# Nine units instead of ten on the first half chunk, and weights split at column 1152

## The chip, the cores and the metric

The kernel runs on one core of one Trainium2 chip. The core has five engines that run their own instruction streams and meet at semaphores: PE (TensorE, matmuls and transposes into PSUM), ACT (ScalarE, activations and PSUM reads), DVE (VectorE, elementwise work and statistics), POOL (GpSimd) and SP (SyncE, which here only issues DMA). The metric is the device time of one execution in microseconds. Before the change it was 170.09 us, the median of 3 runs (169.66 to 171.05).

## The reference

With S = 2048 rows, D = 512 columns and an inner width of 1792, all in bf16:

```python
xn = (x - mean(x)) / sqrt(var(x) + 1e-5)            # over the 512 columns
A  = irfft2(rfft2(xn) * (w_r + 1j * w_i))           # over rows and columns
B  = (gelu(xn @ w_gate) * (xn @ w_up)) @ w_down     # 512 -> 1792 -> 512
out = x + A + B
```

A is a filter in the frequency domain, computed here by matmuls with cosine and sine tables and by elementwise folds. B is a gated feed-forward layer, and holds most of the matmuls.

## The kernel before, in words

**Tiling.** Row r of the kernel's text is a tile of 128 rows of x with all 512 columns; there are 16. Four of them are a chunk b (512 rows), so there are four chunks. A unit is one group of 128 of the 1792 inner columns, numbered fc = 0 to 13. For a unit and a chunk `gated` (L679 and on) computes the gate product g and the up product u, each as four matmuls over the 512 input columns (L688), then gelu of g on ACT (L693), a copy of u on ACT (L696), and their product hT on DVE (L699). `down` (L746) multiplies hT by w_down, 14 matmuls for each row of a chunk. For chunks 0 to 2 ACT and DVE add it into x (L754, L755); for the last chunk DVE adds it from PSUM (L757), and the result is stored.

**The first chunk.** It can't be computed whole at once, since its rows arrive one by one. Rows 0 and 1 are its first half, rows 2 and 3 its second. `by_rows` (L702 and on; matmuls L712, ACT L730 and L731, DVE L732) computes units for one row at a time, 128 columns per matmul, so that a row can begin before the next one is there. The first half is: units 0 to 2 row by row (rows 0 and 1), then units 3 to 9 with both rows at once (256 columns per matmul). The second half is units 0 and 1 row by row (rows 2 and 3), then units 2 to 9 with 256 columns. Units 10 to 13 follow with all four rows at once (512 columns). `NHALF` is the number of units that are done in halves, `NFIRST` (3) of them row by row at the start.

**PSUM.** The gu pool has three banks; a gated unit takes one for g and one for u. In `by_rows` a unit holds g and u in one bank, from gu or from the dn bank, which `down` uses later. The sp pool has two pairs of banks for transposes and spectral products, and for the last chunk's down products.

**Transposes.** The normalized row has to be transposed (xnT) to be a matmul operand. Rows 0 and 1 are transposed on PE (L542, L525). From row 2 on, `turn_dma` (L554) issues a transposing DMA on SP's queue once DVE has written the normalized row (L512). `mirror` (L569) transposes one more tile per chunk in the same way. `fold` builds the operands of the forward transform on DVE; PE transforms over columns at L596 with ACT evicting at L601, over tokens at L834 and L838, back at L915 and L916, and L975.

**The loads.** All on SP's queue in this order: rows 0 to 3, then w_gate and w_up by column ranges (384 to 768, 768 to 1024, 1024 to 1280; columns 0 to 384 come on ACT's queue), the transposes of rows 2 and 3, rows 4 to 7, the transpose of `mirror`, weights 1280 to 1792, rows 8 to 11, a table, rows 12 to 15, and later w_down and the rest. A packet is the run of one weight row, so 256 columns give 512 bytes, 384 give 768 and 512 give 1024.

**The planner.** The order of each engine's instructions is not written out by hand. `_Sched.run` simulates the kernel with fixed costs per operation when the program is built, and lists, for each engine, the operation that can start first, with keys and due times to break ties. DMAs share one pipe of 340 GB/s that starts at 3.3 us, with 0.4 us to land; some early landings are written in. Matmuls of the feed-forward part have keys in program order and fill PE wherever nothing else is ready. PE's spectral operations count as ready 1 us late (`MARGIN`). An `order` list forces one operation behind another on the same engine: ACT evicts the third by-rows unit (dn bank) behind the gelu of units 3 and 5. Nothing is reordered when the program runs.

Of the kernel before, what the change touches and what calls it, by code (L numbers as in the profile page):

```python
# [14 lines left out]
FF = 1792  # L15
P = 128
NFC = 14
NHALF = 10
NFIRST = 3
WARM = 10 * (512,) + (256,)  # L20
HKEY = 1.5
# [123 lines left out]
class _Sched:  # L145
# [11 lines left out]
    def op(self, eng, cost, fn, reads=(), writes=(), tiles=(), key=0.0, after=(), dma=0, lag=0.0, due=None, land=None):  # L157
        o = _Op()
        o.eng, o.fn, o.cost, o.key, o.dma, o.lag, o.due, o.land = eng, fn, cost, key, dma, lag, due, land
        o.reads, o.writes, o.tiles = reads, writes, [(t, False) for t in tiles]  # L160
        o.extra = [a for a in after if a is not None]
        o.order = []
        o.seq = len(self.ops)
        o.end = None
        o.pos = None
        self.ops.append(o)
        return o
# [165 lines left out]
def bass_parallel_sum__spectral_gfnet__glu_gated_geglu__prompt_kernel(  # L333
# [17 lines left out]
    wgv = B_w_gate.rearrange("(dc p) f -> p dc f", p=P)  # L351
    wuv = B_w_up.rearrange("(dc p) f -> p dc f", p=P)
# [5 lines left out]
    with ExitStack() as es:  # L358
        def sb(name, shape, dt=BF16, cell=0):
            n = int(np.prod(shape))  # L360
            t = es.enter_context(nc.sbuf_tensor(name, [P, n], dt))
            return view(t, name, 0, shape, cell)
# [15 lines left out]
        wg = sb("wg", [4, FF])  # L378
        wu = sb("wu", [4, FF])
# [39 lines left out]
        def gub(t, n=512):  # L419
            return ps_gu[:, t.slot * 512:t.slot * 512 + n]  # L420
# [8 lines left out]
        def mm(n):  # L429
            return max(0.0565, n * 0.000421)  # L430

        def c_tt(n):
            return 0.07 + n / 1920.0
# [4 lines left out]
        def c_act(n):  # L438
            return 0.05 + n * 0.00088
# [23 lines left out]
        def load(q, dst, src, nbytes, **kw):  # L463
            return dma(q, dst, lambda: src, nbytes, wr=(dst,), **kw)

        def wload(q, dst, src, lo, hi, **kw):
            return load(q, dst[:, :, lo:hi], src[:, :, lo:hi], (hi - lo) * 1024, **kw)

        k = iter(np.arange(0.0, 1.0, 0.001))
        def rows(lo, hi, land=None):  # L470
            return load("sp", x[:, lo:hi], xb[:, lo:hi, :], (hi - lo) * 131072, key=next(k), land=land)
# [6 lines left out]
        gate.append(warms[3])  # L478
        rows(2, 3, 6.9)
        rows(3, 4, 7.2)  # L480
        for lo, hi in ((384, 768), (768, 1024), (1024, 1280)):
            for w, v in ((wg, wgv), (wu, wuv)):
                wload("sp", w, v, lo, hi, key=next(k))
        op("pool", 0.1, lambda e: e.memset(eps.ap, LN_EPS), writes=(eps,), key=-2)
# [136 lines left out]
        gate.append(early)  # L621
        rows(4, 8)
        k = iter(np.arange(1.0, 2.0, 0.001))
        for w, v in ((wg, wgv), (wu, wuv)):
            wload("sp", w, v, 1280, FF, key=next(k))
        rows(8, 12)
        load("sp", small[:, 1:9].rs([8 * P]), c_small.ap()[:, P:], 262144, key=next(k))
        rows(12, 16)
# [46 lines left out]
        def fkey():  # L675
            fill[0] += 1
            return 1000.0 * fill[0]

        def gated(b, fc, lo, n):  # L679
            h = hs.setdefault((b, fc), _T("hT"))  # L680
            g, u = _T("gu"), _T("gu")
            gs, us = _T("gg"), _T("uu")
            sl = slice(lo // P, (lo + n) // P)

            def f(e, w, t):
                ins = None
                for dc in range(4):
                    ins = e.matmul(gub(t, n), w.ap[:, dc, fc * P:(fc + 1) * P], xnT.ap[:, b, sl, dc, :], start=(dc == 0), stop=(dc == 3))  # L688
                return ins

            for w, t in ((wg, g), (wu, u)):
                op("pe", 4 * mm(n), lambda e, w=w, t=t: f(e, w, t), reads=(w[:, :, fc * P:(fc + 1) * P], xnT[:, b, sl]), tiles=(t,), key=fkey(), lag=0.1)
            o = op("act", c_act(n), lambda e: e.activation(gg.ap[:, gs.slot, 0:n], gub(g, n), ACT.Gelu_apprx_tanh), tiles=(g, gs), key=0.0)  # L693
            if b + lo == 0 and fc in (NFIRST, NFIRST + 2):
                spare[(fc - NFIRST) // 2].order.append(o)
            o = op("act", c_act(n), lambda e: e.activation(uu.ap[:, us.slot, 0:n], gub(u, n), ACT.Copy), tiles=(u, us), key=0.0)  # L696
            if b + lo == 0 and fc == NFIRST:
                o.order.append(spare[0])
            op("dve", c_tt(n), lambda e: e.tensor_tensor(hT.ap[:, h.slot, lo:lo + n], gg.ap[:, gs.slot, 0:n], uu.ap[:, us.slot, 0:n], MUL),  # L699
               tiles=(gs, us, h), key=HKEY)  # L700

# [60 lines left out]
                o = op("sp", 0.41, lambda e, s=s, v=v: e.dma_start(ob[:, s, lo:lo + w], v.ap), reads=(v,), dma=256 * w, key=0.0)  # L762
                sch.finals.append(o)

        spare = by_rows(range(NFIRST), 0, 2)
        filler = []
        for fc in range(NFIRST, NHALF):
            filler.append(("g", 0, fc, 0, 256))
        filler.append(("r", range(2), 2, 1))
        for fc in range(2, NHALF):  # L770
            filler.append(("g", 0, fc, 256, 256))
        for fc in range(NHALF, NFC):
            filler.append(("g", 0, fc, 0, 512))
# [7 lines left out]
        for it in filler:  # L781
            if it[0] == "g":
                gated(*it[1:])
            elif it[0] == "r":
                by_rows(*it[1:])
            else:
                down(*it[1:])

# [238 lines left out]
```

## Time and profile before

| | |
|---|---|
| median of 3 runs | 170.09 us |
| the profiled execution's own time | 170.26 us |
| its span, first to last instruction | 168.6 us |
| granted TensorE clock | 1.00 throughout |
| PE, DVE, ACT, POOL busy | 98%, 86%, 63%, 6% |
| matmuls in gated (L688), down (L746) | 488 and 238 |
| HBM read, written | 11.38 MB, 2.10 MB |
| mean DMA rate over the span | 95 GB/s |

Times in the profile are microseconds from the span's start. Busy times are summed per engine; a matmul's end is modelled and overlaps the next one's start, so the spacing of starts tells what a matmul costs in a row of them. The page's chain is followed back from the last instruction to whatever released each step. A timeline line is: start, length, engine, line, operation, output and inputs, shapes, count, and in brackets the idle time before it and what ended it. A line of the windows view is: stretch, its length, busy time and instructions of PE, PE's weight loads, DVE, ACT and POOL, the granted clock, the DMA engines' mean busy share and GB/s. The trace also holds each DMA packet with its start, length and size, and for each transfer the times at which its 16 parts landed.

### The profile page before, as it was taken

The page shows a single profiled execution, that of the slowest core. Times are in us where ns is not written, and L with a number is a line of the kernel's source. Part 1 is how long each engine was busy: PE and PEld are TensorE (multiplying, and loading weights), DVE is VectorE, ACT ScalarE, POOL GpSimd, SP SyncE. Part 2 cuts the span into 40 slices and gives each one's busy share as a digit, 9 for nine tenths or more (in the row PEclk, how much of TensorE's full clock was granted, in tenths as well). Part 3 has the DMA queues.
Part 4 walks back from the last instruction along what each step waited for, and adds up shares of the span by engine and source line. Part 5 has one row for each costly group of instructions (what it writes and reads, how often), then busy time and mean ns, then how long its engine had stood idle before and what let it go on. Part 6 is the DMA issues. An engine that isn't in the chain of part 4 may idle for free.

```text
span 168.6 us, 2774 instructions
## 1 busy us (share of the span) xinstructions
PE 165.2 (98%) x1035; PEld 88.3 (52%) x1035; DVE 145.8 (86%) x294; ACT 106.5 (63%) x182; POOL 10.3 (6%) x25
## 2 busy tenths in 40 slices
PE   8899999999999999999999999999999999999995
PEld 2698874444554644344444446455444456544443
DVE  2784999999839399999999999999999995999932
ACT  3596977774893956769494639669556399762000
POOL 2040232520000000001000000000000000000000
DMA  5999998895650626425000000000000000033312
GB/s 137 342 294 190 318 289 98 255 290 109 152 116 7 138 85 123 77 72 189 2 0 4 0 0 0 0 4 0 0 2 0 0 0 4 0 124 128 126 62 62
DMA packets 24927, 16.02 MB, mean 95 GB/s; under 512 B 10957, under 2 KB 24274, under 8 KB 24914
## 3 DMA queue, kind: packets, MB, share of 16 engines
q1 hardware_dynamic: 23714, 15.03, 36.3%
q10 hardware_dynamic: 1200, 0.82, 1.5%
q8 instruction: 8, 0.13, 0.4%
q14 instruction: 5, 0.04, 0.1%
HBM read 11.38 MB, written 2.10 MB: 80 GB/s over the span
## 4 chain that ended last, share of the span: by engine, by line
PE 95%; DMA 2%; DVE 1%; SPq 0%; issue 0%; DVEq 0%
PE ps_gu L688 55%; PE ps_dn L746 22%; PE ps_sp L746 7%; PE ps_sp L975 2%; PE ps_sp L596 2%; PE ps_gu L712 2%; DMA x_sb<-in_A_x_dram 2%; PE ps_sp L834 2%; PE ps_sp L915 1%; PE ps_dn L712 1%; PE ps_sp L916 1%; DVE bst L495 0%; PE ps_sp L838 0%; SPq L445 0%; DVE xnT L550 0%
## 5 line engine op out<-in xcount | busy, mean ns | idle before, releaser
L688 PE MATMUL ps_gu<-xnT,wg 128*128 128x512 bf16 (+1 forms) x244 | 55.9, 353 | 0.0
L688 PE MATMUL ps_gu<-xnT,wu 128*128 128x512 bf16 (+1 forms) x244 | 55.9, 353 | 0.0
L696 ACT ACTIVATE uu<-ps_gu 128x512 bf16<-128x512 f32 (+1 forms) x61 | 33.8, 555 | 11.9 <-PE ps_gu L688 11.3
L693 ACT ACTIVATE gg<-ps_gu 128x512 bf16<-128x512 f32 (+1 forms) x61 | 33.8, 555 | 10.1 <-PE ps_gu L688 8.1
L746 PE MATMUL ps_dn<-wd,hT 128*128 128x512 bf16 x168 | 39.0, 379 | 0.0
L688 PEld LDWEIGHTS ps_gu<-xnT,wu 128*128 128x128 bf16 x244 | 23.6, 98 | 21.3
L449 DVE TENSOR_TENSOR specB<-specB 128x512 bf16<-128x512 bf16 (+2 forms) x58 | 33.3, 611 | 0.7 <-ACT specB L980 0.5
L688 PEld LDWEIGHTS ps_gu<-xnT,wg 128*128 128x128 bf16 x244 | 23.4, 98 | 20.0
L699 DVE TENSOR_TENSOR hT<-gg,uu 128x512 bf16<-128x512 bf16 (+1 forms) x61 | 23.0, 384 | 5.0 <-ACT uu L696 4.7
L746 PEld LDWEIGHTS ps_dn<-wd,hT 128*128 128x128 bf16 x168 | 16.3, 98 | 19.5 <-issue 0.4
L754 ACT ACTIVATE db<-ps_dn 128x512 bf16<-128x512 f32 x12 | 7.2, 597 | 19.9 <-PE ps_dn L746 19.9
L495 DVE BATCH_NORM_STATS2 bst<-x_sb 128x6 f32<-128x512 bf16 x16 | 10.9, 684 | 3.5 <-DMA x_sb<-in_A_x_dram 3.4
L449 DVE TENSOR_TENSOR specC<-specB 128x1024 bf16<-128x1024 bf16 (+2 forms) x18 | 12.5, 714 | 0.3
L746 PE MATMUL ps_sp<-wd,hT 128*128 128x512 bf16 (+2 forms) x70 | 12.3, 336 | 0.0
L449 DVE TENSOR_TENSOR specB<-specA 128x2048 bf16<-128x2048 bf16 x8 | 9.4, 1220 | 2.3 <-ACT specA L601 2.3
L746 PEld LDWEIGHTS ps_sp<-wd,hT 128*128 128x128 bf16 x70 | 6.4, 98 | 6.1 <-DVE x_sb L757 0.2
L449 DVE TENSOR_TENSOR specB<-specB,filt 128x2048 bf16<-128x2048 bf16 x8 | 9.4, 1222 | 0.0
L843 ACT ACTIVATE specA<-ps_sp 128x1024 bf16<-128x1024 f32 x8 | 8.0, 1037 | 1.0 <-PE ps_sp L838 1.0
L980 ACT ACTIVATE specB<-ps_sp 128x1024 bf16<-128x1024 f32 x8 | 8.0, 1036 | 0.1
L921 ACT ACTIVATE specC<-ps_sp 128x1024 bf16<-128x1024 f32 x8 | 7.8, 1042 | 0.0
L601 ACT ACTIVATE specA<-ps_sp 128x1024 bf16<-128x1024 f32 x8 | 7.8, 1033 | 0.0
L449 DVE TENSOR_TENSOR specA<-specB 128x2048 bf16<-128x2048 bf16 (+1 forms) x8 | 7.6, 986 | 0.1
(68 smaller groups left out, 128.6 us busy)
## 6 DMA issues: line engine op xcount, KB each, us to landing
out_dram<-x_sb SPq DMA_DIRECT2D x15, 128.0 KB, 1.8
wd<-in_B_w_down_dram SPq DMA_DIRECT2D x1, 1792.0 KB, 8.2
x_sb<-in_A_x_dram SPq DMA_DIRECT2D x3, 512.0 KB, 7.0
toki<-c_ti SPq DMA_DIRECT2D x1, 768.0 KB, 4.3
tokf<-c_tf SPq DMA_DIRECT2D x1, 576.0 KB, 4.2
x_sb<-in_A_x_dram SPq DMA_DIRECT2D x4, 128.0 KB, 3.7
wg<-in_B_w_gate_dram SPq DMA_DIRECT2D x2, 256.0 KB, 6.5
wu<-in_B_w_up_dram SPq DMA_DIRECT2D x2, 256.0 KB, 6.3
```

The costliest lines, as they stand in the source:

```text
L449: return op("dve", c_tt(n), lambda e: e.tensor_tensor(o.ap, a.ap, b.ap, f), reads=(a, b), writes=(o,), key=key, **kw)
L495: op("dve", 0.61, lambda e: e.bn_stats(bst[:, s].ap, xs(s).ap), reads=(xs(s),), writes=(bst[:, s],), key=key, due=due, after=after)
L601: op("act", c_act(1024), lambda e, yv=yv, t=t: e.activation(yv.ap, spair(t).rearrange("p (s r i) -> p s i r", s=4, r=4), ACT.Copy), writes ...
L688: ins = e.matmul(gub(t, n), w.ap[:, dc, fc * P:(fc + 1) * P], xnT.ap[:, b, sl, dc, :], start=(dc == 0), stop=(dc == 3))
L693: o = op("act", c_act(n), lambda e: e.activation(gg.ap[:, gs.slot, 0:n], gub(g, n), ACT.Gelu_apprx_tanh), tiles=(g, gs), key=0.0)
L696: o = op("act", c_act(n), lambda e: e.activation(uu.ap[:, us.slot, 0:n], gub(u, n), ACT.Copy), tiles=(u, us), key=0.0)
L699: op("dve", c_tt(n), lambda e: e.tensor_tensor(hT.ap[:, h.slot, lo:lo + n], gg.ap[:, gs.slot, 0:n], uu.ap[:, us.slot, 0:n], MUL), tiles=(g ...
L746: ins = e.matmul(bank(), hT.ap[:, hs[(b, fc)].slot, sl * P:(sl + 1) * P], wd.ap[:, fc, lo:lo + n], start=(fc == 0), stop=(fc == NFC - 1))
L754: op("act", c_act(n), lambda e: e.activation(db.ap[:, d.slot, 0:n], bank(), ACT.Copy), tiles=(t, d), key=0.0)
L843: op("act", c_act(1024), lambda e, xv=xv, t=t: e.activation(xv.ap, spair(t), ACT.Copy), writes=(xv,), tiles=(t,), key=-0.5)
L921: op("act", c_act(1024), lambda e, gv=gv, t=t: e.activation(gv.ap, spair(t).rearrange("p (k x i) -> p k x i", k=4, x=4), ACT.Copy), writes ...
L980: op("act", c_act(1024), lambda e, rv=rv, t=t: e.activation(rv.ap, spair(t), ACT.Copy), writes=(rv,), tiles=(t,), key=-0.5)
```

## The change

`NHALF` goes from 10 to 9, so unit 9 is done once with all four rows and no longer in two halves. The second half's row-by-row part takes three units with two gu banks and dn, as the first half's does; before, it took two units with one gu bank and dn. The ACT orderings behind the gelu of units 3 and 5 hold for both halves. The weight columns ahead of the transposes end at 1152 instead of 1280, in two ranges instead of three; the rest follows in two ranges, 1152 to 1408 and 1408 to 1792, instead of one.

```diff
-NHALF = 10
+NHALF = 9
...
-        for lo, hi in ((384, 768), (768, 1024), (1024, 1280)):
+        for lo, hi in ((384, 768), (768, 1152)):
             for w, v in ((wg, wgv), (wu, wuv)):
                 wload("sp", w, v, lo, hi, key=next(k))
...
-        for w, v in ((wg, wgv), (wu, wuv)):
-            wload("sp", w, v, 1280, FF, key=next(k))
+        for lo, hi in ((1152, 1408), (1408, FF)):
+            for w, v in ((wg, wgv), (wu, wuv)):
+                wload("sp", w, v, lo, hi, key=next(k))
...
-            if b + lo == 0 and fc in (NFIRST, NFIRST + 2):
-                spare[(fc - NFIRST) // 2].order.append(o)
+            if (b, n) == (0, 256) and fc in (NFIRST, NFIRST + 2):
+                spare[lo][(fc - NFIRST) // 2].order.append(o)
...
-            if b + lo == 0 and fc == NFIRST:
-                o.order.append(spare[0])
+            if (b, n) == (0, 256) and fc == NFIRST:
+                o.order.append(spare[lo][0])
...
-        spare = by_rows(range(NFIRST), 0, 2)
+        spare = {0: by_rows(range(NFIRST), 0, 2)}
...
-        filler.append(("r", range(2), 2, 1))
-        for fc in range(2, NHALF):
+        filler.append(("r",))
+        for fc in range(NFIRST, NHALF):
             filler.append(("g", 0, fc, 256, 256))
...
-                by_rows(*it[1:])
+                spare[256] = by_rows(range(NFIRST), 2, 2)
```

## The prediction

> **What bounds the kernel now.** I read the page's busy shares first, then the chain that ended last, then TensorE's timeline, then the transfers around the only hole in it.
>
> ```profile
> span 168.6 us, 2774 instructions
> PE 165.2 (98%) x1035; PEld 88.3 (52%) x1035; DVE 145.8 (86%) x294; ACT 106.5 (63%) x182; POOL 10.3 (6%) x25
> PE 95%; DMA 2%; DVE 1%; SPq 0%; issue 0%; DVEq 0%
> ```
>
> PE is busy 98% of the span and is 95% of the chain, so the time is PE's work plus the holes in it. I looked for the holes by comparing successive matmul starts with the usual spacing. After the first transposes (5.5 us) there are 1.01 us of them in all: 0.43 around the row-0 transposes, which the change doesn't touch; 0.21 at 15.23; and 0.10, 0.10 and 0.13 at 69.8, 70.4 and 137.0. The hole at 15.23, with the last unit of the first half and the first of the second:
>
> ```profile
> 14.36 0.60 PE L688 MATMUL ps_gu<-xnT,wg 128*128 128x256 bf16 x4
> 14.79 0.60 PE L688 MATMUL ps_gu<-xnT,wu 128*128 128x256 bf16 x4
> 15.44 0.38 PE L712 MATMUL ps_gu<-xnT,wg 128*128 128x128 bf16 x4
> 15.66 0.39 PE L712 MATMUL ps_gu<-xnT,wu 128*128 128x128 bf16 x4
> ```
>
> Groups start 0.437 us apart, so the next was due at 14.79 + 0.437 = 15.23 and came at 15.44. It needs row 2 transposed. In the trace's landing records that transfer, issued at 10.31, completed at 15.30 (5.0 us later); row 3, issued at 11.67, at 15.65. The same transfer on empty queues, issued at 39.67, 40.98 and 42.29, completed at 42.19, 43.48 and 44.79: 2.50 us. The waits view names ACT for this hole, but the bank in question was freed at 14.95, so it was the transfer. Why it was late is seen in the queue and in the DMA column (last two numbers: share, GB/s):
>
> ```profile
> 7.25 1.47 SPq L445 DMA_DIRECT2D wu<-in_B_w_up_dram  x1
> 10.31 2.61 SPq L554 DMA_TRANSPOSE xnT<-specB  x2
> ...
> 11.50:12.00 0.50, 0.50 (x7) 0.44 (x6) 0.50 (x4) 0.45 (x3) 0.00 (x0) 1.00 1.21 291
> 13.00:13.50 0.50, 0.50 (x7) 0.44 (x6) 0.27 (x1) 0.45 (x2) 0.00 (x0) 1.00 1.14 247
> 13.50:14.00 0.50, 0.50 (x7) 0.46 (x5) 0.02 (x1) 0.45 (x2) 0.00 (x0) 1.00 2.51 31
> 14.50:15.00 0.50, 0.50 (x7) 0.46 (x5) 0.03 (x1) 0.40 (x3) 0.00 (x0) 1.00 0.13 22
> ```
>
> Weights run until 12.7; the two transposes' 256-byte packets run from 11.9 to 13.6; then almost nothing moves until 15.0. Inside lies an instruction fetch: one packet of 16384 bytes on queue q8 at 13.01, 1.16 us long. The engine that carries it serves its last transpose packets from 14.18 to 14.98, and only then do row 2's completion writes, begun at 13.6, come through. So the hole has two causes, weights ahead and a fetch in the middle.
>
> **The sum, part by part.** *PE's work.* Unit 9 goes from two halves, 4 x 0.437 = 1.748 us, to one whole, 2 x 0.864 = 1.728 (groups at 24.21 and 25.07). Unit 2's second half goes from 0.874 to row by row, 16 matmuls at 56 ns (eight in 0.45 us in the chain) = 0.894. Sum 0.00.
>
> *The hole.* The first half loses 0.874 us, so PE comes to row 2 at 15.23 - 0.87 = 14.36 and needs it landed by 14.23 (landing to matmul took 15.30 to 15.44). Ahead of the transposes, 1024 packets of 768 bytes replace 2048 of 512. Their mean times in the trace are 40 and 33 ns; over 16 engines that is 2.56 instead of 4.22 us, and the skipped pair 1024 to 1280 no longer holds SP for 1.58 and 1.47 us. By the landings it is a little less: 384 KB transfers land 1.23 us apart (8.57, 9.80), so the last weights land at 9.80 + 2 x 1.23 = 12.26, not 13.27. The transposes' issue stays at 10.31, since it waits for row 2's norm on DVE (9.88 + 0.41). Bounds for row 2: 10.31 + 2.50 = 12.81 with free queues, 15.30 if nothing helps. I take 12.8, because the weights' packets are then through by about 11.6, where the transposes' first can start (issue + 1.25 at 40.9), and its completion precedes the fetch, which comes at PE's 103rd matmul and so stays near 13.0. Row 3 stays behind the fetch: 15.0 to 15.65, due at 14.36 + 6 x 0.224 - 0.13 = 15.57; 0 to 0.08 us. The hole of 0.21 goes.
>
> *New waits at the front.* wu to column 1152 lands at 12.26; unit 6's up group runs at 12.17 in the trace. In the old order it would start at 12.40: +0.23. The planner's own figure for that landing is 12.28 (3.3 us, 2.92 MB at its 340 GB/s, 0.4), and where it saw such a wait before it put the gate groups first (12 matmuls at 9.12, then 12 up matmuls at 10.43). I take 0, bound +0.23. Row by row with three units takes two gu banks and dn; counted from the second half's start T, the nearest thing to a wait is unit 5's gate group at T + 4.44, whose bank (unit 3's up, copied behind unit 2's gelu) is free at about T + 4.31. Cost 0; if ACT is later, some 0.1.
>
> *Loads behind.* The second batch is 256 KB larger and in smaller packets: 1024 of 512 and 1024 of 768 bytes at 33 and 40 ns instead of 1024 of 1024 at 47, over 16 engines 4.67 instead of 3.01 us. Two more issues of 0.5 us also lie ahead of rows 8 to 15 on SP; the queue then waits for DVE until 21.20 anyway. So rows 8 to 11 land up to 1.66 us after 23.55, at 25.21, and row 8's statistics on DVE (24.07) wait up to 1.1 us. Queued behind them are hT products (gg and uu have four slots; DVE is two to three units behind, so PE isn't reached) and the norms of rows 6 and 7, then their transposes, then wd (landed 36.92, first used 39.75, so 1.2 us remain). PE's forward token transforms have room: z ready 40.5, used 42.93; 45.9 and 47.28; 53.7 and 55.4. DVE's idle stretches of 0.72 at 43.60 and 1.61 at 49.98 take up lag. Cost 0.
>
> The Trainium skill, in "DMA: Bandwidth & Descriptors" (Why small descriptors are slow), gives a packet a fixed cost of about 3 cycles beside 32 bytes per cycle. By that rule, as an estimate, the second batch would take 3.01 x 46/35 = 3.95 us, so rows 8 to 11 would be 0.94 late and not 1.66. The trace's 33, 40 and 47 ns contain about 19 ns per packet, a larger share than the page's, and I keep the rows.
>
> **Total.** The profiled run was 170.26 us (span 168.6, 1.66 around it): 170.26 - 0.21 = 170.05. The median of the three runs shown is 0.17 lower, so I forecast 169.9. Three runs between 169.66 and 171.05 can't tell this from no change; about 1% could be told.
>
> **Rivals.** *Row 2 lands no earlier* (slower; 12%). The transposes can't start before 11.6, and if the fetch still catches row 2's completion it lands at 15.30. PE would start the second half at 15.44 with unit 9's half still ahead: +0.87, 170.96. It decides at a landing of 14.43; any later is slower than before. For it: today's 13.6 to 15.0. Against it: 1.0 us less in the queue, and completion writes at 13.6 today would come near 12.7, ahead of the fetch. The Trainium skill, "Runtime: NRT & Kernel Launch" (Instruction fetch mechanics), calls crossing a 16 KiB block of instructions mostly hidden; by that this rival would have no place, while the trace shows 1.4 us in which transposes waited.
>
> *The lag reaches PE by way of DVE* (22%). DVE's long spectral part begins when ACT has the last forward transforms, runs nearly without a hole, and ends just before PE needs its result:
>
> ```profile
> 49.98 0.69 DVE L449 TENSOR_TENSOR specB<-xnT 128x1024 bf16<-128x1024 bf16 x1 [1.61 <-DMA xnT<-specB]
> 58.01 2.36 DVE L449 TENSOR_TENSOR specB<-specA 128x2048 bf16<-128x2048 bf16 x2 [2.27 <-ACT specA L601]
> ...
> 159.66 0.69 DVE L757 TENSOR_TENSOR x_sb<-ps_sp,x_sb 128x512 bf16<-128x512 f32 x1
> ```
>
> The third down product of the last chunk takes the bank that this L757 frees at 160.35, and starts at 160.69: 0.34 us of room. The planner's transfers shift by about +0.22 (0.77 for 256 KB, less 0.55 saved ahead), and it places transforms between groups of 0.86 us, so about one time in four one moves back a group. Then DVE starts 0.86 - 0.21 later and PE stalls 0.65 - (0.34 - 0.21) = 0.52: 169.9 + 0.5 = 170.4. If all 1.66 us came through, 169.9 + 1.66 - (0.34 - 0.21) = 171.4. Against it: the 2.27 us at 58.01 are a wait for PE's own order, not for loads.
>
> *A new order of the planner with a stall above 1.7 us* (5%): about 172; nothing in the profile asks for it.
>
> *Much faster* (2%): the holes from 15.23 on are 0.54 us together, so over 1% has no source in the profile.
>
> **How the numbers follow.** The forecast, 59%, with its own range 169.4 (the other 0.33 us of holes gone too, and noise) to 170.3 (unit 6 waits, row 3 waits). Adding the first rival and most of the second gives 169.4 to 171.1. Over 1% faster 2%, slower 5%, within 93%.
>
> **What would show it.** Right: L712's second run starts at 14.3 to 14.5, right behind unit 8; row 2 lands near 12.8; row 8's statistics wait for x_sb; wd is in before the first down product. Wrong: a hole ahead of that run up to 15.4 (first rival); a hole before L834, L975 or the last L746 (second). The least sure step is the fetch: another place of that one packet moves a transpose by more than a microsecond.

## The result and the profile after

Over 22 executions each on one chip, the kernel before took 170.1 us (median; 169.66 to 171.66) and the changed kernel 171.05 us (170.21 to 173.07). The ratio is 1.0050, with a 95% interval of 1.0029 to 1.0072: half a per cent slower. Two executions of the changed kernel, at 172.89 and 173.07 us, count as slow and are left out of the ratio. I had forecast 169.9 us, a gain of 0.2; the measured change is a loss of 0.95. 171.05 lies outside the forecast's own range (169.4 to 170.3) and inside that of the second rival (170.4 to 171.4). The profiled execution of the changed kernel took 171.52 us, 1.26 us more than that of before. Its page begins:

```profile
span 169.9 us, 2757 instructions
PE 165.0 (97%) x1023; PEld 87.5 (52%) x1035; DVE 145.6 (86%) x293; ACT 105.9 (62%) x180; POOL 10.1 (6%) x25
...
PE 50%; DVE 18%; SPq 15%; DMA 13%; issue 2%; ACT 1%; POOL 0%; POOLq 0%
```

PE's busy time is the same (165.0 against 165.2). But in the chain that ended last PE's share has fallen from 95% to 50%; followed backwards, the chain now leaves PE for DVE, for SP's queue and for the loads. PE's work is not longer: PE waits more. (1023 matmuls against 1035 weight loads means that 12 matmul records are missing. Each shows as a spacing that is 0.216 us too long; such spacings are not holes and are left out below.)

The hole at 15.23 is gone, as the timeline of PE in the changed kernel shows. Unit 8 is followed by the second half without a break:

```profile
13.64 0.60 PE L689 MATMUL ps_gu<-xnT,wu 128*128 128x256 bf16 x4
14.08 0.39 PE L713 MATMUL ps_gu<-xnT,wg 128*128 128x128 bf16 x4
...
15.19 0.39 PE L713 MATMUL ps_dn<-xnT,wu 128*128 128x128 bf16 x4
15.64 0.40 PE L713 MATMUL ps_gu<-xnT,wg 128*128 128x128 bf16 x4
```

14.08 lies 0.44 behind 13.64, the usual spacing. The next break is between the last two lines: 15.64 is 0.45 behind 15.19 where 0.22 is usual, so 0.23 us are lost at the first matmul of row 3. I listed all holes after the first gated matmul in both traces by comparing successive starts with the usual spacing:

| place | before | after | PE waits for |
|---|---|---|---|
| second half | 0.21 (row 2) | 0.23 (row 3) | transposing DMA |
| 23.1 | 0 | 0.50 | ACT, which waits for DVE |
| 31.4 | 0 | 0.52 | row 7's transpose |
| 70 | 0.19 | 0.20 | unchanged |
| 102, 106 | 0 | 0.31, 0.15 | DVE, behind the filter loads |
| 137 | 0.13 | 0.13 | unchanged |
| sum | 0.53 | 2.03 | |

The holes account for 1.50 us more. PE's first gated matmul was at 5.89 instead of 6.17, because row 1 of x happened to land sooner, which takes 0.28 off: +1.22 against a span that grew by 1.25. So PE lost nothing elsewhere in this execution; the question is where each new hole comes from, and whether it is there in every execution or only in some.

**The hole at 23.** Timelines of PE, then ACT, then DVE of the changed kernel:

```profile
22.23 1.03 PE L689 MATMUL ps_gu<-xnT,wg 128*128 128x512 bf16 x4
23.59 0.82 PE L689 MATMUL ps_gu<-xnT,wu 128*128 128x512 bf16 x3 [0.33 <-ACT gg L694]
```

```profile
21.56 0.38 ACT L697 ACTIVATE uu<-ps_gu 128x256 bf16<-128x256 f32 x1
23.15 0.38 ACT L694 ACTIVATE gg<-ps_gu 128x256 bf16<-128x256 f32 x1 [1.21 <-DVE hT L733]
```

```profile
15.62 0.69 DVE L449 TENSOR_TENSOR specB<-xnT 128x1024 bf16<-128x1024 bf16 x1 [1.51 <-DMA xnT<-specB]
...
21.24 0.41 DVE L512 TENSOR_SCALAR specB<-x_sb,bag,rstd 128x512 bf16<-128x512 bf16 x1 [0.31 <-POOL rstd L508]
21.56 0.18 DVE L496 BATCH_NORM_AGGREGATE bag<-bst 128x2 f32<-128x6 f32 x1
21.66 1.26 DVE L449 TENSOR_TENSOR specC<-specB 128x1024 bf16<-128x1024 bf16 x2
22.83 0.28 DVE L733 TENSOR_TENSOR hT<-gg,uu 128x256 bf16<-128x256 bf16 x1
```

Read it from the bottom. L733 at 22.83 is the product of the third by-rows unit. In DVE's order it stands behind a norm, an aggregate and two folds (z). Until it is done, the gg slot of that unit is taken, so ACT's next gelu waits 1.21 us, its PSUM bank stays full, and PE's up group starts 0.50 us late. DVE had also idled 1.51 us for row 3's transpose before 15.62. That alone doesn't account for the hole: the statistics of row 4 began at 17.43 and couldn't have begun before their rows, which landed at 17.05. By this trace, as an estimate with these rows landing where they did, row 3 in time would have brought the product forward by 0.38 us at most, and 0.12 of the 0.50 would stay.

**The hole at 31.** Timelines of PE in the kernel before and in the changed one, then of DVE in the same order:

```profile
31.11 1.03 PE L688 MATMUL ps_gu<-xnT,wg 128*128 128x512 bf16 x4
31.89 0.82 PE L689 MATMUL ps_gu<-xnT,wg 128*128 128x512 bf16 x3 [0.35 <-DMA xnT<-specB]
```

```profile
24.07 0.69 DVE L495 BATCH_NORM_STATS2 bst<-x_sb 128x6 f32<-128x512 bf16 x1
25.61 0.69 DVE L495 BATCH_NORM_STATS2 bst<-x_sb 128x6 f32<-128x512 bf16 x1 [0.88 <-DMA x_sb<-in_A_x_dram]
```

PE waits for row 7's transpose, which landed at 31.84; before, it landed at 29.98, and the group came at 31.11. Behind this are the loads: rows 8 to 11 landed at 25.59 instead of 23.55. DVE's statistics of row 8 waited 0.88 us for them, and the norms of rows 6 and 7, which are behind the statistics of rows 8 and 9 in the new order, ran at 27.08 instead of 24.76 and 25.36.

**The holes at 102 and 106.** DVE in the kernel before, DVE in the changed one, then PE there:

```profile
79.85 0.50 DVE L882 TENSOR_TENSOR edge<-specA,edge 128x16 bf16<-128x16 bf16 x2 [0.18 <-ACT gg L693]
```

```profile
81.04 0.18 DVE L883 TENSOR_TENSOR edge<-specA,edge 128x16 bf16<-128x16 bf16 x1 [0.59 <-POOL edge L849]
81.42 0.18 DVE L883 TENSOR_TENSOR edge<-specA,edge 128x16 bf16<-128x16 bf16 x1 [0.20 <-POOL edge L849]
```

```profile
101.75 1.03 PE L689 MATMUL ps_gu<-xnT,wg 128*128 128x512 bf16 x4
102.93 0.23 PE L916 MATMUL ps_sp<-toki,specA 128*128 128x128 bf16 x1
```

POOL prepares the edge columns from the filter, whose last load landed at 81.18 instead of 79.94, since SP issued these loads from 54.32 instead of 52.55 on (they are gated on the last chunk's fold). From 81.04 on DVE's spectral part runs nearly without a hole, and 0.79 us of waiting there come out as 0.46 us on PE 21 to 25 us later.

### The profile page after: what moved, and what is told of

Same layout as the page of the kernel before. It is cut to its first block, busy times and chain, and to the rows that moved or that the text cites. A ratio compares the mean times of both kernels' runs of the same rounds, so it can differ in the third digit from the quotient of the medians.

```text
span 169.9 us, 2757 instructions
## 1 busy us (share of the span) xinstructions
PE 165.0 (97%) x1023; PEld 87.5 (52%) x1035; DVE 145.6 (86%) x293; ACT 105.9 (62%) x180; POOL 10.1 (6%) x25
## 4 chain that ended last, share of the span: by engine, by line
PE 50%; DVE 18%; SPq 15%; DMA 13%; issue 2%; ACT 1%; POOL 0%; POOLq 0%
PE ps_gu L689 26%; SPq L445 14%; PE ps_dn L747 10%; DVE specB L449 10%; PE ps_sp L747 7%; DMA x_sb<-in_A_x_dram 6%; DMA xnT<-specB 5%; PE ps_sp L976 2%; DMA filt<-in_A_w_r_dram 2%; DVE bst L495 2%; DVE hT L700 2%; DVE specC L449 1%; DVE specA L449 1%; PE ps_sp L916 1%; PE ps_gu L713 1%
## 5 line engine op out<-in xcount | busy, mean ns | idle before, releaser
L689 PE MATMUL ps_gu<-xnT,wg 128*128 128x512 bf16 (+1 forms) x236 | 55.0, 357 | 0.4 <-DMA xnT<-specB 0.4
L689 PE MATMUL ps_gu<-xnT,wu 128*128 128x512 bf16 (+1 forms) x236 | 55.0, 357 | 0.3 <-ACT gg L694 0.3
L694 ACT ACTIVATE gg<-ps_gu 128x512 bf16<-128x512 f32 (+1 forms) x59 | 33.1, 563 | 12.0 <-PE ps_gu L689 9.7
L697 ACT ACTIVATE uu<-ps_gu 128x512 bf16<-128x512 f32 (+1 forms) x59 | 33.1, 562 | 11.8 <-PE ps_gu L689 11.4
L747 PE MATMUL ps_dn<-wd,hT 128*128 128x512 bf16 x157 | 37.0, 379 | 0.7 <-issue 0.2
L689 PEld LDWEIGHTS ps_gu<-xnT,wu 128*128 128x128 bf16 x236 | 22.8, 98 | 21.9 <-ACT gg L694 0.8
L689 PEld LDWEIGHTS ps_gu<-xnT,wg 128*128 128x128 bf16 x236 | 22.6, 98 | 21.2 <-DMA xnT<-specB 0.8
L449 DVE TENSOR_TENSOR specB<-xnT 128x1024 bf16<-128x1024 bf16 (+1 forms) x8 | 4.2, 553 | 4.3 <-DMA xnT<-specB 4.3
```

The lines of the kernel that those rows point to most:

```text
L449: return op("dve", c_tt(n), lambda e: e.tensor_tensor(o.ap, a.ap, b.ap, f), reads=(a, b), writes=(o,), key=key, **kw)
L747: ins = e.matmul(bank(), hT.ap[:, hs[(b, fc)].slot, sl * P:(sl + 1) * P], wd.ap[:, fc, lo:lo + n], start=(fc == 0), stop=(fc == NFC - 1))
```

## Experiments

All were timed against the kernel before on the same chip. "Holes" are those of PE in the profiled execution, as in the table above, without those at 70 and 137. The lowest time is over 5 to 12 executions (22 for after). Before's lowest lay between 169.64 and 169.68 in every batch.

| run | ratio, 95% | median, lowest | holes |
|---|---|---|---|
| after | 1.0050 [1.0029, 1.0072] | 171.05, 170.21 | 0.23 row 3; 0.50 at 23; 0.52 at 31; 0.31 and 0.15 at 102 |
| k1 two units | 1.0057 [1.0032, 1.0082] | 170.80, 169.80 | 0.48 row 3; 0.08 at 31; 0.39 at 83; 0.97 and 0.14 at 102 |
| k2 old weights | 1.0025 [1.0001, 1.0049] | 170.68, 169.63 | 0.89 row 2 |
| k3 third unit only | 1.0019 [1.0001, 1.0036] | 170.24, 169.68 | 0.06 at 23 |
| k4 nine units only | 1.0022 [1.0002, 1.0042] | 170.57, 169.69 | 0.90 row 2 |
| x1 before, small packets | 0.9992 [0.9978, 1.0005] | 169.86, 169.70 | 0.18 row 2 |
| x3 after, one range | 1.0040 [1.0028, 1.0053] | 170.51, 170.22 | 0.36 row 3; 0.50 at 23 |
| x4 after, norms first | 1.0034 [1.0013, 1.0055] | 170.53, 169.77 | 0.48 row 3; 0.39 at 31; 0.08 at 105 |
| y1 after, filter early | 1.0040 [1.0026, 1.0054] | 170.54, 170.18 | 0.48 row 3; 0.49 at 23 |
| f1 after, warm-up split | 1.0038 [1.0023, 1.0053] | 170.67, 170.51 | 0.32 row 3; 0.50 at 23; 0.12 at 31 |
| f2 after, row 3 on PE | 1.0053 [1.0038, 1.0069] | 170.84, 170.51 | 1.39 at 12.6 |
| f3 before, warm-up split | 1.0007 [0.9995, 1.0019] | 170.07, 169.82 | 0.21 at 19.7 |
| c1 after, f1 + x3 + y1 | 1.0032 [1.0013, 1.0050] | 170.57, 170.19 | 0.05 row 3; 0.29 at 23 |
| g1 after, three mends | 1.0000 [0.9989, 1.0011] | 170.00, 169.68 | none |
| g3 after, told of row 3 | 1.0013 [0.9996, 1.0030] | 170.08, 169.69 | 0.27 row 3 |
| g4 g3 + one range + filter early | 1.0018 [1.0000, 1.0036] | 170.08, 169.77 | 0.17 row 3 |
| y2 before, filter early | 0.9993 [0.9977, 1.0009] | 169.82, 169.69 | none |

### The parts of the change, each alone or missing

k4 sets `NHALF` to 9 in the kernel before; k3 gives that kernel the third by-rows unit in the second half and keeps 10; k2 has both and the old weight ranges; k1 is the changed kernel with two units by rows. For k2:

```diff
-        for lo, hi in ((384, 768), (768, 1152)):
+        for lo, hi in ((384, 768), (768, 1024), (1024, 1280)):
...
-        for lo, hi in ((1152, 1408), (1408, FF)):
-            for w, v in ((wg, wgv), (wu, wuv)):
-                wload("sp", w, v, lo, hi, key=next(k))
+        for w, v in ((wg, wgv), (wu, wuv)):
+            wload("sp", w, v, 1280, FF, key=next(k))
```

> The changed kernel with two units instead of three row by row in the second half (one gu bank and dn, as before); nine units on the first half and the new weight ranges stay. Theory 1 (late loads: the larger second batch of weights in smaller packets lands rows 8 to 15 some 2 us later, so the transposes of rows 4 to 7 end after 31 us and chunk 1 waits for them): the loads are the same, so the time stays at 0.5% over the kernel before, about 171.0 us, and rows 4 to 7 are transposed at 31 to 32 us. Theory 2 (the planner's new DVE order: statistics of rows 8 and 9 ahead of the norms of rows 6 and 7): that order is the same here, so also 171.0. Theory 3 (the third row-by-row unit: its hT product comes late, ACT has no gg slot and PE stalls 0.5 us at 23): that hole goes, and the time is about 170.5 us.

> The changed kernel with the old weight ranges (ahead of the transposes to column 1280 in three ranges, the rest in one). Theories 1 and 2: rows 8 to 15 land as before (23.5 and 25.6 us), the DVE order is again statistics of row 8, norms of rows 6 and 7, statistics of row 9; but row 2 lands at 15.3 us as before while PE is there at 14.4, so a hole of about 1.1 us opens at the front: 0.9 us more than the kernel before, about 171.0 us. If the front hole were not there (row 2 at 13), the time would be that of the kernel before. Theory 3: 171.0 plus up to 0.5 us for a hole behind the by-rows units.

> The kernel before with only the third row-by-row unit in the second half (ten units on the first half, old weight ranges). Theories 1 and 2: loads as before, order nearly as before: no change, 170.1 us within 0.2. Theory 3 (the third unit by rows costs a hole of its own): 170.4 to 170.6 us, with a hole on PE behind the by-rows units at about 22 to 24 us and ACT waiting for an hT product.

> The kernel before with only nine instead of ten units on the first half (two units by rows, old weight ranges). All theories: PE reaches row 2 at 14.4 us and waits for its transpose until 15.3, 0.87 us more than before, so about 171.0 us. If the transposes of rows 4 to 7 (landed at 30.0 before) leave PE less room than I think, nothing more is added, since PE is later and not earlier there.

Without the new weight ranges the shorter first half meets a late row 2. The timeline of PE in k2:

```profile
13.61 0.60 PE L688 MATMUL ps_gu<-xnT,wu 128*128 128x256 bf16 x4
14.94 0.38 PE L712 MATMUL ps_gu<-xnT,wg 128*128 128x128 bf16 x4 [0.73 <-DMA xnT<-specB]
```

Row 2 landed at 14.80 there and at 14.98 in k4; in the changed kernel it landed at 12.57. This is what my first rival described, a late row 2 with unit 9's half still ahead. It had put the hole at 1.08 (PE there at 14.36, the group at 15.44); the holes found are 0.89 and 0.90, because row 2 landed a little sooner than the 15.30 it took. It is paid only where the weights stay as they were, and not each time: k4's twelve times lie at 169.69 to 170.08 (four) and 170.55 to 170.94 (eight), about 0.86 apart. So the medians, 170.68 and 170.57, are below the 171.0 that I expected of both.

So the new ranges do what I had expected for row 2, and the loss is elsewhere. k1 has no hole at 23 and its lowest time is within 0.14 us of that of before: that hole belongs to the third unit together with the rest. By itself the third unit costs little: k3, with ten units and the old ranges, has a hole of 0.06 there and a median of 170.24, within 0.2 of the 170.1 that theories 1 and 2 gave. But k1 loses as much by the median, at 102 above all. The views of DVE and of PE's waits in k1:

```profile
81.39 0.18 DVE L883 TENSOR_TENSOR edge<-specA,edge 128x16 bf16<-128x16 bf16 x1 [1.67 <-POOL edge L849]
```

```profile
PE ps_sp L916 <- DVE specA L883: 0.8, 1, 0.8
```

1.67 us of DVE's wait for the filter's edges are 0.97 us on PE. There is more than one source of loss, then.

### Loads: packets, ranges and the filter

x1 is the kernel before with its second weight batch in two ranges of 256 columns (512-byte packets), x3 the changed kernel with that batch as one range, y1 the changed kernel with the filter loads gated on the norm of row 15 instead of on the last chunk's fold. The order of operations on PE, DVE, ACT and POOL stays as it was in all three, by their traces. x3 and y1:

```diff
-        for lo, hi in ((1152, 1408), (1408, FF)):
+        for lo, hi in ((1152, FF),):
```

```diff
-        gate.append(turned[3])
+        gate.append(hold[15])
```

> The kernel before with the second batch of weights (columns 1280 to 1792) in two ranges of 256 columns instead of one of 512: the same bytes in 512-byte packets and two more issues, and DVE, ACT and PE in the same order as before. By the packets' 33 and 47 ns rows 8 to 15 land about 1.2 us later. Theory 1 (late loads): everything behind them on SP's queue moves back by 0.5 to 1.2 us, the transposes of rows 4 to 7 and the filter loads among them; the filter loads end near 81 instead of 79.9 us, DVE's small edge products wait for them, and the time goes to 170.5 to 171.0 us. Theory 2 (the planner's new DVE order is the cause, not the loads): the order is that of before, so 170.0 to 170.2 us.

> The changed kernel with the second batch of weights (1152 to 1792) in one range of 640 columns instead of two: the same bytes in packets of 1280 bytes, two issues fewer, and DVE, ACT and PE in the same order as in the changed kernel. By about 54 ns per packet the batch takes 3.5 instead of 4.7 us, so rows 8 to 15 land 1.2 us earlier. Theory 1: most of the loss goes, 170.2 to 170.6 us. Theory 2: the order is unchanged, so 170.9 to 171.1 us.

> The changed kernel with the filter loads no longer held back until fold(3) is partly done, but only until the norm of row 15: SP issues them about 7 us earlier. DVE, ACT and PE have the same order as in the changed kernel. It leaves the wait of chunk 1 for rows 4 to 7 (about 0.5 us in the profile) and takes away DVE's wait for the filter at its edge products (0.8 us at 81). If the filter loads carry the loss into DVE's chain: 170.2 to 170.7 us, no idle DVE at 81 and no hole on PE at 102. If only chunk 1's wait counts: 171.0 us.

x1 cost nothing: the last part of rows 8 to 11 landed at 23.55, as before (the first at 22.25 instead of 21.96), so it didn't make the rows late as its first theory supposed, and couldn't show what late rows cost. By their first parts, the loads of 256 KB in 512-byte packets landed 0.77 to 0.86 us apart in x1, and those of 512 KB in 1024-byte packets 1.50 in before. For the 1 MB of the batch that is at most 4 x 0.86 - 2 x 1.50 = 0.4 us more. By adding up packet durations, as I did in the prediction, it would have been 2048 x 33 against 1024 x 47 ns over 16 engines, 1.2 us more. The Trainium skill, in "DMA: Bandwidth & Descriptors" (Why small descriptors are slow), gives 3 cycles per packet beside 32 bytes per cycle; as an estimate that makes 3.0 x 38/35, or 0.26 more. The trace is much nearer to that rule than to my sum.

x3 took rows 8 to 11 back to 23.36 and row 7's transpose to 30.39; the hole at 31 went, and DVE ran both L883 products at 80.04 without a wait, so the ones at 102 went too. y1 took away the wait at 81 and the holes at 102; there was also no hole at 31, with row 7 at 31.07, but PE came later there, behind 0.97 us of holes. The distance of the medians to before, 0.95 us for the changed kernel, is 0.56 for x3 and 0.59 for y1; the intervals overlap with that of the changed kernel, so a gain in time from either alone isn't shown. Both kept the holes of row 3 and at 23, and both stay at 1.004. y2, the same gate in the kernel before, showed that before has nothing to win there:

> The kernel before with the filter loads gated on row 15's norm instead of the last z fold, nothing else. Theory: before has its filter in time (last load 79.94, no wait of VectorE at 81), so nothing is won, ratio 0.999 to 1.001. Rival (the filter's own transfers cost TensorE or VectorE time wherever they land): a change of more than 0.002 either way.

### The fetch and the transposes

Every trace has one packet of 16384 bytes, an instruction fetch (queue q8), between 12 and 17 us, which lasts 0.9 to 1.3 us. The trace doesn't name its engine; I take it for PE's, which has by far the most instructions. In the changed kernel it began at 13.30 and took 1.24 us. Of the 16 parts of row 3's transpose 15 landed at 13.71 to 13.86, and one at 15.60. That this one lies on the DMA engine with the fetch is my reading, as is "the engine that carries it" in the prediction; the trace doesn't number the engines. f1 and f3 have 17 warm-up matmuls instead of 11, with the same columns in all, to bring the fetch forward; f2 transposes row 3 on PE; c1 is f1 with x3 and y1.

```diff
-WARM = 10 * (512,) + (256,)
+WARM = 4 * (512,) + 13 * (256,)
```

```diff
-            turn_dma(s)
+            if s == 2:
+                turn_dma(s)
+            else:
+                turn(s, 1, -50.0)
```

> The changed kernel with six of the 512-column warm-up matmuls cut into twelve of 256 columns: the same columns and time, six more PE instructions pairs ahead, so the instruction fetch that now begins at 13.3 to 14.0 us begins some 0.7 us earlier. Orders of DVE, ACT and PE behind the warm-up are the same. Theory 4 (the fetch is the root: it holds back one of the 16 parts of row 3's transpose from 13.9 to 15.4 to 16.0 us; PE waits 0.2 to 0.5 us for row 3, and DVE starts chunk 0's folds late, so hT products and the statistics behind them are late too and PE stalls 0.5 us more near 23): row 3 is complete before 15.3 us, the hole behind row 2 goes, the one at 23 shrinks, and the time is 170.0 to 170.5 us. If the fetch can't be moved so or isn't the cause: 170.7 to 171.1 us with the same holes.

> The kernel before with the same warm-up (twelve matmuls of 256 columns for six of 512). Theory 4: row 2's transpose completes earlier than 15.3 us by about as much as the fetch moves (0.5 to 0.7), PE needs it at 15.1, so the hole of 0.2 us ahead of the second half goes: 169.7 to 169.9 us. If the fetch isn't the cause: 169.95 us and the same hole.

> The changed kernel with row 3 transposed on PE (four transposes, 0.22 us, and a copy of 0.42 us on DVE) as row 1 is, and not by a transposing DMA. This takes away what makes row 3 late and costs PE 0.22 us; the planner's DVE order changes with it. Theory 4: no hole behind row 2 and none at 23, so 170.0 to 170.4 us. Theories 1 and 2 (loads behind, statistics ahead of norms): these stay, so 170.8 to 171.2 us.

> The changed kernel with three things together: the earlier fetch (warm-up as above), the second batch of weights in one range of 640 columns, and the filter loads held back only until the norm of row 15. If the fetch, the late loads and the filter path are all of the loss, PE has no hole over 0.1 us after 6 us but those at 70, and the time is that of the kernel before less its own hole: 169.7 to 169.9 us, the best of all. If something else remains: 170.2 us or more.

The fetch didn't go where I wanted it: 13.60 in f1, and in f3 16.67, later instead of earlier. As tests of its effect they still serve, since each time the transfer that it met was late:

| kernel | fetch at | late transfer | parts in time | parts late |
|---|---|---|---|---|
| before | 13.01 | row 2's transpose | none | 16, 15.06 to 15.30 |
| after | 13.30 | row 3's transpose | 15, 13.71 to 13.86 | 1, 15.60 |
| f1 | 13.60 | row 3's transpose | 15, 13.86 to 14.03 | 1, 15.79 |
| f3 | 16.67 | rows 4 to 7 | 1, 17.12 | 15, 18.48 to 18.54 |
| f2 | 12.00 | w_up 768 to 1152 | 13, 11.14 to 11.57 | 3, 13.79 to 13.84 |

How many parts are late differs, and the runs don't say why; a transfer counts as landed when its last part has. In f3 nothing stands in the way of the transposes: row 2 landed at 13.75 (15.30 before) and row 3 at 14.22, and the second half began without a hole. DVE then waited for rows 4 to 7, and PE lost the 0.21 us there (timelines of DVE and PE in f3):

```profile
18.56 0.69 DVE L495 BATCH_NORM_STATS2 bst<-x_sb 128x6 f32<-128x512 bf16 x1 [1.79 <-DMA x_sb<-in_A_x_dram]
```

```profile
19.33 0.60 PE L688 MATMUL ps_gu<-xnT,wg 128*128 128x256 bf16 x4
19.98 0.61 PE L688 MATMUL ps_gu<-xnT,wu 128*128 128x256 bf16 x4
```

In f2 the up group of a first-half unit waited for its weights (timeline of PE in f2):

```profile
13.97 1.03 PE L692 MATMUL ps_gu<-xnT,wu 128*128 128x256 bf16 x8 [1.23 <-DMA wu<-in_B_w_up_dram]
```

That is the largest hole of all, and after it f2 has none but those at 70. The late transfer changes with the time of the fetch. I have no version without it, so that it is the cause of the late parts rests on these five coincidences and isn't shown; what sets its time stays open too. c1, with the split warm-up, the one range and the early filter, stayed at 1.0032: what is left in its profile is above all the 0.29 at 23.

### DVE's order

x4 forces DVE's order in the changed kernel: norms of rows 6 and 7 ahead of the statistics of rows 8 to 11, the two z folds behind the statistics of row 7. g1 is x4 with x3's range and y1's gate. g3 leaves the order to the planner, but tells it that row 3's transpose lands 1.2 us later than it had assumed; g4 is g3 with x3's range and y1's gate. x4's core and g3:

```diff
+        for s in range(8, 12):
+            stat[s].order += [hold[6], hold[7]]
+        for o in zs[0]:
+            o.order.append(stat[7])
```

```diff
-... key=-5.0, lag=-0.4 if s < 4 else 0.0)
+... key=-5.0, lag=(0.8 if s == 3 else -0.4) if s < 4 else 0.0)
```

> The changed kernel with DVE's order put back by hand towards that of the kernel before: the norms of rows 6 and 7 ahead of the statistics of rows 8 to 11, and the last two folds of chunk 0 behind the statistics of row 7. Loads unchanged. Theory 2: the transposes of rows 6 and 7 are issued about 1.5 us earlier, chunk 1 doesn't wait, and the time is 170.1 to 170.4 us. Theory 1: these transposes only queue longer behind rows 12 to 15 (landed at 27.6), and the filter loads stay late, so 170.7 to 171.1 us.

> The changed kernel with three mends at once: norms of rows 6 and 7 ahead of the statistics of rows 8 to 11 and the last z folds of chunk 0 behind the statistics of row 7 on VectorE, the second weight batch as one range of 640 columns, and the filter loads gated on row 15's norm. Theory (the holes at 23, 31 and 102 us are separate losses, each with its own cause, and row 3's transpose stays): all three holes gone, one hole of 0.3 to 0.5 left at 15.4 in place of before's 0.21, so 0.1 to 0.3 us above before, ratio 1.0005 to 1.002. Rival (the loss lies elsewhere, or VectorE's lag comes out at the next place): ratio stays at 1.003 to 1.004 with a hole at a new place.

> The changed kernel with the planner's landing time of row 3's transpose set 1.2 us later, near where it lands on the chip; TensorE's order stays the same, VectorE takes the half-chunk products ahead of chunk 0's fold and no longer idles for the transpose. Theory (the hole at 23 comes from VectorE idling 1.5 us for row 3 and then running products late): hole at 23 gone, row 3's hole at 15.4 and possibly those at 31 and 102 stay, ratio 1.001 to 1.003. Rival (order doesn't matter, the products are late for another reason): hole at 23 stays near 0.5, ratio 1.004 to 1.005.

> The changed kernel with the planner told of row 3 as in the other run, one range of 640 columns in the second weight batch and the filter loads gated on row 15's norm. Theory: only row 3's hole of 0.3 to 0.5 left, 0.1 to 0.3 us above before, ratio 1.0005 to 1.002, the same as with the forced order on VectorE. Rival: 1.003 to 1.004, the loss is not in these holes.

By their traces x4, g1 and g3 run the same operations in the same order as the changed kernel on PE, ACT and POOL. DVE's order differs, in x4 only from the third product on, and SP's in an issue or two behind 40 us. x4 alone removed the hole at 23, although row 3 landed later than in the changed kernel (15.87): its third product ran at 21.93, ahead of the folds. So with row 3 as late as this, it is DVE's order that makes the hole. No run has the changed kernel's order with row 3 in time; the estimate above gives 0.12 us for it. x4's median, 170.53, lies between what the two theories gave. The hole at 31 stayed (0.39): x4 keeps the two ranges, rows 8 to 11 landed at 24.81, and the transposes of rows 4 to 7, which are behind the loads in the queue, from 29.57 to 31.48.

g1 brings everything back. Its page, its list of waits of PE (one line in all, a warm-up matmul), and ACT and DVE at the place of the old hole:

```profile
span 168.0 us, 2765 instructions
PE 165.3 (98%) x1035; PEld 88.0 (52%) x1035; DVE 145.4 (87%) x293; ACT 105.9 (63%) x180; POOL 10.4 (6%) x25
```

```profile
PE ps_dn L458 <- PEq L1020: 0.8, 1, 0.8
```

```profile
21.37 0.38 ACT L704 ACTIVATE uu<-ps_gu 128x256 bf16<-128x256 f32 x1
21.82 0.38 ACT L701 ACTIVATE gg<-ps_gu 128x256 bf16<-128x256 f32 x1
```

```profile
21.47 0.26 DVE L740 TENSOR_TENSOR hT<-gg,uu 128x256 bf16<-128x256 bf16 x1
...
22.98 1.28 DVE L449 TENSOR_TENSOR specC<-specB 128x1024 bf16<-128x1024 bf16 x2
```

The third unit's product (L740 here) is at 21.47 instead of 22.83, the z folds follow at 22.98, and ACT goes on without a wait. Only 0.19 us of holes are left, those at 70, and PE started at 5.89: 0.53 - 0.19 + 0.28 = 0.62 less than before's profile, and the span is 0.6 shorter (168.0). y2, with the front of before, came to the same 168.0 with the same 0.19. So with these stalls mended the changed kernel ties, at 1.0000 [0.9989, 1.0011]. That is better than the 1.0005 to 1.002 expected. In the profile row 3 landed at 15.41, in time for PE at 15.46, which is luck and none of the three mends. I have no version that beats the kernel before. g1 also tells the parts apart by time: x4, which lacks the range and the gate, is at 1.0034 [1.0013, 1.0055], and c1, which lacks the order (and has the split warm-up), at 1.0032 [1.0013, 1.0050]. Both intervals lie clear of g1's: with the order mended, range and gate together still bring 0.34%, and with range and gate mended, the order still brings 0.32%. The two are more than the whole loss of 0.50%, so the parts don't simply add up.

g3 shows the same by another way: told where row 3 lands, the planner itself puts DVE's work in an order that leaves no hole at 23 (third unit's product at 21.75), and none at 31 or 102 in the profile. It keeps the two ranges and rows 8 to 11 still landed late, at 24.68, but row 7's transpose landed at 30.19: late loads alone don't make those holes either. g3's 1.0013 is at the lower end of its expectation. g4's 1.0018 lies in its range, but is no better than g3, and its profile has only 0.17 for row 3. What g4's slower executions (up to 171.24) lose isn't seen in its profile.

The lowest times separate the always from the sometimes. Kernels whose profile has a hole of 0.49 or 0.50 at 23 have a lowest time of 170.18 to 170.51 (after, x3, y1, f1); c1, with 0.29, 170.19. Those changed kernels without it, k1, x4, g1, g3 and g4, have 169.68 to 169.80; f2, with its 1.39 elsewhere, is the exception at 170.51. The difference, about 0.5 us, is the size of the hole, so I take it that the hole is in every execution of the changed kernel, and that the rest of the 0.95 us lost in the median comes and goes with landing times. Neither is shown: each kernel has one profile, c1 fits the first less well, and k1, without the hole, still lost 0.83 us in the median.

## Why the prediction was wrong, step by step

Two terms that the sum put at nothing failed: the third by-rows unit, and the loads behind. Row 3's wait was mis-sized. What the sum said of PE's work and of row 2 came true. The holes of before that it starts from, 1.01 us, add up to 0.97 by its own parts; nothing else rests on that figure.

**PE's work, 0.00.** Right: 165.0 us busy against 165.2, with 12 records missing; g1, with the same matmuls and all records, has 165.3.

**Row 2, landing 12.8; its hole of 0.21 gone.** Right: 12.57, which is 2.54 after its issue at 10.03; the second half began at 14.08 behind unit 8, where 14.36 less the 0.28 of PE's earlier start was due. The reason was right as well, fewer weights ahead and a completion before the fetch; k2 and k4 show what it could have cost otherwise. The gain was smaller than the profile of before suggested, however: y2 and k3, with before's weights ahead of the transposes, had no hole there either. I took a hole seen in one execution as one that is always there.

**Row 3, 0 to 0.08 us.** Mechanism right, size too small: 0.23 in the profile, 0.17 to 0.48 in k1, x3, x4, y1, f1, g3 and g4, but 0.05 or less in c1 and g1. The landing was 15.60 (15.40 to 16.04 in those), in the late half of my 15.0 to 15.65 or behind it. With PE 0.28 sooner it was due at row 3 at 15.42 and not at 15.70, and the term was mis-sized by that lead.

**Unit 6's weights, 0.** Right: w_up to 1152 landed at 12.06, and the planner put gate groups first.

**Three by-rows units: "Cost 0; if ACT is later, some 0.1".** This step failed. For it I checked PSUM banks only. The third unit also has a product on DVE, and until that is done it holds one of the four gg and uu slots. The planner put the product behind a norm, an aggregate and two folds: 0.50 us at 23 in the profile, and by the lowest times probably in every execution. In x4 the order on PE and ACT is the same and DVE's is another from this product on, and the hole is gone.

**Loads behind, "Cost 0".** This step failed too. Rows 8 to 11 landed at 25.59, beyond the bound of 25.21, for more reasons than the packets: +2.04 us. SP issued the batch 0.34 later (15.67), since the issue of `mirror`'s transpose ahead of it took 2.30 us instead of 1.68; the first part of rows 8 to 11 took 1.25 us longer from there (I had 1.66 for this, and 0.94 as the estimate by the Trainium skill's rule); the last part was 0.45 further behind the first. What failed above all is "cost 0". I wrote that norms 6 and 7 and their transposes would wait, and followed them to w_down, where there was room (landed 38.74, 1.8 us later than before). I didn't follow them to chunk 1's first gate group, which had 29.98 to 31.11, 1.13 us of room, and lost 0.52.

**The rivals.** The third way into the loss, the filter, was in none of them: SP issued the filter loads 1.77 us later, and DVE stood 0.79 us for the edges. y1, which issues them sooner, took that wait and the holes at 102 and 106 away. The second rival, lag that reaches PE by way of DVE (170.4 to 171.4), is what happened in kind, but not at the place I gave it: not at 58.01, and not by a transform that moves back a group. That 171.05 lies in its range is luck, since its price was worked out for that other place. I gave it 22%, because I looked for DVE's lag only behind its idle stretches at 43 to 58 and took "DVE is two to three units behind, so PE isn't reached" as enough for the units before. At 23, 31 and 102 an engine off the path kept a slot, a queue or an operand that PE needed soon.

**The fetch.** As the forecast had it, the fetch kept its place (13.30), row 2's completion was ahead of it and row 3's behind it. The Trainium skill, "Runtime: NRT & Kernel Launch" (Instruction fetch mechanics), calls the crossing of a block mostly hidden. For PE's own instructions the traces show nothing against that. For the transfers beside it they do, as far as the fetch is the cause: the late parts in its table came 1.4 to 2.3 us behind those in time.

## What to carry to other kernels

When an edit adds a unit of work ahead of an engine's queue, list every buffer that it holds until its last consumer, on each engine, and look at where that consumer stands in the new order: bank counts alone said 0 and the slot in SBUF cost 0.5 us in the profile. When loads move, follow each to its first use on the critical engine and write the room beside it; here a room of 1.13 us at chunk 1's first group was too small, and the filter's place in the queue wasn't looked at. And where a planner orders the work from assumed landing times, correct those with the landings in the trace before judging the edit: here one number (1.2 us for row 3) brought the ratio from 1.0050 to 1.0013 without touching the change.

## What the runs showed of the hardware

- A transfer is as late as its slowest part: 15 of 16 parts of row 3's transpose had landed at 13.86 and the last came at 15.60, with a 16 KB instruction fetch of 1.24 us begun at 13.30. Which transfer was late went with the time of the fetch, 12.0 to 16.7 us in these kernels; that the fetch is the cause is likely and not shown. Going from 11 warm-up matmuls to 17 with the same columns moved it from 13.01 to 16.67 in the kernel before (f3) and from 13.30 to 13.60 in the changed one (f1). I can't say why.
- Durations of packets overlap. 512-byte and 1024-byte packets last 33 and 47 ns in the trace, but loads made of them ran at 0.77 to 0.86 us per 256 KB (x1) and 1.50 us per 512 KB (before): half-size packets cost 15% at most, not 40%.
- PE's first gated matmul began at 5.86 to 6.17 us in these kernels. Between before and after the 0.28 us are row 1's landing (4.20 against 3.79), for which DVE waited 0.35 in before; in k4 (6.03) row 1 was in time and the start was late all the same. A lead of this kind was lost again at row 3's transpose in the changed kernel (0.23).
